# A fused linear-attention and GEGLU kernel: weight loads held back behind the DMA transposes, a re-ordered start, and four PSUM tensors for the last output tiles

## The chip, the cores and the metric

The kernel runs on one core of a Trainium2 chip. The metric is device time in microseconds (us) of one execution. "Before" and "after" are always run on the same chip in alternating rounds. An execution is slow when it takes over 1.5% more than the fastest of the same kernel in those rounds. A ratio below compares the fast runs of the two kernels in the same rounds, so it is not quite the ratio of the medians or means that are quoted beside it.

Engines in the profile: PE (matmuls) and PEld (loading of the stationary operand), DVE (vector), ACT (scalar), POOL (GpSimd, which also issues the plain loads here), SP (which issues the transposing loads and the stores).

## The reference, cut to what matters

```python
x = A_x                                            # [1, 2048, 640] bf16
g = sigmoid((x * gate_w).sum(-1, keepdims=True))
q, k, v = split_heads(x @ wqkv)                    # 32 heads of 20
phi(t)  = concat(softmax(t @ w_phi), softmax(-(t @ w_phi)))
a = (phi(q) @ (phi(k).T @ v)) / (phi(q) @ sum(phi(k)) + 1e-6) @ wo
b = (gelu(x @ w_gate) * (x @ w_up)) @ w_down       # inner width 1728
out = g * a + (1 - g) * b
```

## The kernel before

The kernel has five stages. The change touches the first and the last.

1. Start. `w_phi` is folded into the q and k weights, so that later one matmul gives `x @ Wq @ w_phi`. For this the weights are needed transposed (`wkT`, `wqT`; ten transposing DMAs on SP's queue), together with a block-diagonal matrix `BD` that PE builds from `w_phi`. `x` is transposed on PE (`xT`).
2. K/V loop over 16 tiles of 128 tokens. 3. phi(q). 4. GEGLU, 56 blocks. The output tiles of all but the last 512 tokens are made between GEGLU blocks.
5. Tail: the last four output tiles.

The loads, all issued in one go at the start (cuts are marked `...`):

```python
for k in range(NC_):   # 5 DMA transposes, then 5 more for wqT, on SP's queue
    emit_dma("sp", lambda e, k=k: e.dma_start_transpose(wkT[:, k, :], A_wqkv[:, 640+128*k : 640+128*(k+1)]), sem=s_wkT)
...
# POOL's queue, in this order: WPH, XR (x, 2 halves), masks, W1v, then without any wait
for g in range(NG):
    emit_dma("pool", lambda e, g=g, gr=gr: e.dma_start(Wo[0:gr, g, :], A_wo[120*g:120*g+gr, :]), sem=s_wo)
emit_dma("pool", ... Wgt ...); emit_dma("pool", ... Wup ...); emit_dma("pool", ... Wd ...)
```

The work of PE in the start, in program order:

```python
bd_ring = _Ring(K, "bd", 1, ["dve"])      # one PSUM slot: PA
for k in range(NC_): ...                  # BD block k: matmuls into PA, two DVE copies out
emit_xt_items(NC_ * NTG)                  # all 20 items of xT: 4 transposes, one copy (ACT or DVE)
emit_fold(wkT, W1k, extra_waits=[wkT_wait] + bd_done)   # 5 blocks of 10 matmuls, ACT copies
emit_fold(wqT, W1q, extra_waits=[wqT_wait])
```

The output tiles. Each tile `t` is: 28 "down" matmuls (`Ddown`) into PD; ACT scales PD into BSB; 12 `Wo` matmuls (`DA`) into the same PD; DVE combines PD and BSB; store.

```python
def pe_Ddown(T, tt):  w = a_ring.prod_waits(t)      # waits for DVE of the tile before
    ... e.matmul(PD[:, c0:c1], lhsT=hT[...], rhs=Wd[...])
def pe_DA(T, tt):     w = [bsb_ring.cons_wait(t)]   # waits for ACT's copy of this tile
    ... e.matmul(PD[:, c0:c1], lhsT=oT[...], rhs=Wo[...])
```

The softmax here doesn't subtract the row's maximum and nothing guards it: scores larger than these inputs give would overflow.

## Time and profile before

| | |
|---|---|
| time, median of the first 4 runs | 443.08 us (438.36 to 446.39) |
| profiled execution | 446.13 us, span 444.4 |
| first matmul of the K/V loop | 67.58 us |
| PE waits for `wqT` | 25.6 us in one piece |
| last `hT` (GEGLU done) ends | 408.98 us |
| from there to the end | 35.4 us |

The page's second part shows the span in 40 slices of 11.1 us. Digits are busy tenths; PEclk is the granted matmul clock in tenths; DMA is the mean busy share of the 16 DMA engines. Before:

```profile
PE   0681049999979989889999999999999999997875
PEclk9997559999989999999999999999999999999899
DMA  8999900000000000000000000000000000000000
```

From 33 to 67 us (digits 1, 0, 4) PE is mostly idle, while the DMA engines are busy up to 55. The chain of waits of the first 70 us (start, duration, what) says for what:

```profile
18.90 3.48 SPq L242
22.42 38.20 DMA wqT<-in_A_wqkv_dram
60.75 1.09 PE PD L388 x10
...
66.49 0.37 PE PC L465
...
67.64 1.48 PE PA L485 x10
```

The last `wqT` transpose is issued at 22.42 and takes 38.20 us to land. Then the q fold (L388) runs and the K/V loop (L485) starts. The list of waits (us in total, times, longest) names the same wait:

```profile
PE PD L388 <- DMA wqT<-in_A_wqkv_dram: 25.6, 1, 25.6
```

The chain at the end: the down matmuls of tile 12, and one whole tile out of four (the short pieces called "issue" between the lines, 0.02 to 0.05 us each, are left out):

```profile
409.12 5.76 PE PD L830 x28
...
426.49 4.09 PE PD L830 x28
430.61 0.80 ACT BSB L843
431.45 1.92 PE PD L854 x12
433.40 0.90 DVE OUT L868
434.34 4.09 PE PD L830 x28
```

A tile lasts 434.34 - 426.49 = 7.85 us and PE works for 6.01 of them. It waits for ACT (0.87) and for DVE (0.96), because all four steps use PD. The first down part took 5.76 us instead of 4.09: the granted clock was 0.5 from 410.0 to 413.4.

### The profile page before, as it was taken

To read this page: it belongs to the slowest core of one execution; us is meant where nothing else is said; L and a number is where in the kernel's file an instruction comes from. 1 tells how busy PE (TensorE), PEld (TensorE's weight loads), DVE (VectorE), ACT (ScalarE), POOL (GpSimd) and SP (SyncE) were. 2 spreads that over 40 slices of the span, in tenths; PEclk is the share of its full clock that TensorE was granted. 3 is DMA by queue.
4 is the path that set the end of the run, shared out by engine and by line. 5 is a ranking of instruction groups with operands and counts; after the bars stand their busy time and mean duration, and the time that the engine had idled before them with its cause. 6 is when DMAs were issued, how large, how long until landed. Compare 5 with 4: busy or idle time off the path is not lost.

```text
span 444.4 us, 5682 instructions
## 1 busy us (share of the span) xinstructions
PE 377.8 (85%) x2232; PEld 187.4 (42%) x2232; DVE 249.6 (56%) x333; ACT 187.2 (42%) x353; POOL 20.9 (5%) x39
## 2 busy tenths in 40 slices
PE   0681049999979989889999999999999999997875
PEld 0471045666644433333344444444444444443332
DVE  0420006999984477788999944557445574445001
ACT  1152034555536554453557744344444344441010
POOL 8900000000000000000000000000000000000000
PEclk9997559999989999999999999999999999999899
DMA  8999900000000000000000000000000000000000
GB/s 234 165 252 348 117 19 0 2 1 2 0 1 0 0 1 0 2 0 0 2 0 0 1 0 17 15 17 15 14 2 16 15 16 15 3 15 31 15 16 30
DMA packets 11434, 15.55 MB, mean 35 GB/s; under 512 B 7442, under 2 KB 9491, under 8 KB 11408
## 3 DMA queue, kind: packets, MB, share of 16 engines
q0 software_dynamic: 2384, 10.93, 8.3%
q1 hardware_dynamic: 9024, 4.26, 6.9%
q8 instruction: 18, 0.29, 0.3%
q14 instruction: 8, 0.07, 0.0%
HBM read 10.92 MB, written 2.62 MB: 30 GB/s over the span
## 4 chain that ended last, share of the span: by engine, by line
PE 66%; DVE 13%; DMA 9%; SPq 5%; issue 5%; ACT 2%; DVEq 0%
PE PD L830 15%; PE PB L754 9%; PE PA L754 9%; DMA wqT<-in_A_wqkv_dram 9%; PE PC L754 8%; PE PD L854 7%; PE PA L602 5%; DVE PHK L526 3%; DVE ZS L519 3%; SPq L242 3%; PE PA L485 3%; SPq L239 2%; DVE PHQ L640 2%; PE PB L629 2%; PE PD L696 2%
## 5 line engine op out<-in xcount | busy, mean ns | idle before, releaser
L830 PE MATMUL PD<-Wd,hT 128*128 128x512 bf16 x448 | 66.8, 304 | 5.6 <-DVE OUT L868 3.9
L808 DVE SCALAR_TENSOR_TENSOR hT<-Th,Pt 128x512 bf16<-128x512 bf16 (+1 forms) x56 | 38.4, 686 | 49.5 <-ACT Th L796 48.5
L843 ACT ACTIVATE BSB<-PD,omg 128x640 f32<-128x640 f32 x16 | 12.7, 793 | 98.8 <-PE PD L830 98.8
L830 PEld LDWEIGHTS PD<-Wd,hT 128*128 128x128 bf16 x448 | 34.6, 99 | 37.7 <-DVE OUT L868 7.2
L754 PE MATMUL PA<-xT,Wgt 128*128 128x512 bf16 (+1 forms) x190 | 47.5, 380 | 0.8 <-DVE Pt L787 0.7
L519 DVE TENSOR_REDUCE ZS<-EK 128x64 f32<-128x1280 bf16 x16 | 23.8, 1486 | 41.2 <-ACT EK L506 41.2
L754 PE MATMUL PC<-xT,Wup 128*128 128x512 bf16 (+1 forms) x185 | 46.0, 379 | 0.0
L868 DVE SCALAR_TENSOR_TENSOR OUT<-PD,gcol,BSB 128x640 bf16<-128x640 f32 x16 | 14.1, 883 | 51.2 <-PE PD L854 51.2
L640 DVE TENSOR_TENSOR PHQ<-EQ,PB 120x1024 bf16<-120x1024 bf16 (+1 forms) x24 | 29.1, 1212 | 12.7 <-PE PB L630 12.7
L796 ACT ACTIVATE Th<-Zt 128x512 bf16<-128x512 bf16 (+1 forms) x56 | 35.2, 631 | 0.0
L854 PE MATMUL PD<-Wo,oT 120*128 120x512 bf16 x192 | 30.4, 300 | 4.4 <-ACT BSB L843 4.4
L770 ACT ACTIVATE U<-PA 128x512 bf16<-128x512 f32 (+1 forms) x38 | 22.6, 595 | 23.4 <-PE PB L754 9.4
L602 PE MATMUL PA<-xT,W1q 128*120 128x512 bf16 (+1 forms) x120 | 31.2, 395 | 0.0
L673 ACT ACTIVATE NTS<-PC 120x512 bf16<-120x512 f32 (+1 forms) x24 | 14.3, 596 | 35.5 <-PE PC L654 35.5
L754 PEld LDWEIGHTS PC<-xT,Wup 128*128 128x128 bf16 (+1 forms) x185 | 18.3, 99 | 21.7
L754 PEld LDWEIGHTS PA<-xT,Wgt 128*128 128x128 bf16 (+1 forms) x190 | 16.7, 98 | 24.4 <-issue 7.9
L787 DVE SCALAR_TENSOR_TENSOR Pt<-PC,Gb 128x512 bf16<-128x512 f32 (+1 forms) x37 | 25.5, 690 | 1.3
L784 DVE SCALAR_TENSOR_TENSOR Zt<-U,PA 128x512 bf16<-128x512 bf16 (+1 forms) x38 | 25.8, 678 | 0.0
L388 PE MATMUL PD<-BD,wqT 128*128 128x120 bf16 (+1 forms) x30 | 3.1, 285 | 25.6 <-DMA wqT<-in_A_wqkv_dram 25.6
L485 PE MATMUL PA<-W1k,xT 128*128 128x512 bf16 (+1 forms) x160 | 24.5, 300 | 0.0
L495 PE MATMUL PB<-W1v,xT 128*128 128x512 bf16 (+1 forms) x160 | 24.5, 300 | 0.0
L526 DVE TENSOR_TENSOR PHK<-EK,RK 128x1280 bf16<-128x1280 bf16 x16 | 23.9, 1491 | 0.6
(114 smaller groups left out, 507.5 us busy)
## 6 DMA issues: line engine op xcount, KB each, us to landing
XR<-in_A_x_dram POOLq DMA_DIRECT2D x2, 1280.0 KB, 9.2
out_dram<-OUT SPq DMA_DIRECT2D x16, 160.0 KB, 1.8
Wgt<-in_B_w_gate_dram POOLq DMA_DIRECT2D x1, 2160.0 KB, 21.6
Wup<-in_B_w_up_dram POOLq DMA_DIRECT2D x1, 2160.0 KB, 35.4
Wd<-in_B_w_down_dram POOLq DMA_DIRECT2D x1, 2080.0 KB, 29.0
W1v<-in_A_wqkv_dram POOLq DMA_DIRECT2D x5, 160.0 KB, 9.9
Wo<-in_A_wo_dram POOLq DMA_DIRECT2D x5, 150.0 KB, 10.5
wkT<-in_A_wqkv_dram SPq DMA_TRANSPOSE x5, 11.3
```

The source lines that it names most:

```text
L485: emit("pe", lambda e, tgt=tgt, c=c, n0=n0, n1=n1, t=t: e.matmul(tgt, lhsT=xT[:, c, 128 * t:128 * (t + 1)], rhs=W1k[:, c, n0:n1], start=(c ...
L519: emit("dve", lambda e, s=s: e.tensor_reduce(ZS[:, s, :], EK[:, s, :, :].rearrange("p i (h d) -> p (i h) d", d=20), axis=AX.X, op=ALU.add) ...
L526: emit("dve", lambda e, s=s: e.tensor_tensor(PHK[:, s, :, :].rearrange("p i (h d) -> p (i h) d", d=20), EK[:, s, :, :].rearrange("p i (h d ...
L602: emit("pe", lambda e, tgt=tgt, c=c, g=g, gr=gr, T=T, last=last: e.matmul(tgt, lhsT=W1q[:, c, 120 * g:120 * g + gr], rhs=xT[:, c, 512 * T: ...
L640: emit("dve", lambda e, g=g, gr=gr: e.tensor_tensor(PHQ[0:gr, g, :, :], EQ[0:gr, g, :, :], PB[0:gr, 0:1024].rearrange("p (i n) -> p i n", ...
L754: emit("pe", lambda e, tgt=tgt, Wsrc=Wsrc, c=c, fc=fc, kr=kr, T=T: e.matmul(tgt, lhsT=Wsrc[:, c, 128 * fc:128 * fc + kr], rhs=xT[:, c, 512 ...
L784: emit("dve", lambda e, kr=kr, s=s, Gp=Gp: e.scalar_tensor_tensor(Zt[0:kr, s, :], U16[0:kr, s, :], K1, Gp, ALU.add, ALU.mult), waits=w, si ...
L787: emit("dve", lambda e, kr=kr, s=s, Up=Up: e.scalar_tensor_tensor(Pt[0:kr, s, :], Up, 0.5, Gb[0:kr, s, :], ALU.mult, ALU.mult), waits=w2, ...
L796: emit("act", lambda e, kr=kr, s=s: e.activation(Th[0:kr, s, :], Zt[0:kr, s, :], ACTF.Tanh), waits=w, sig=th_ring.prod_signal(j))
L808: emit("dve", lambda e, kr=kr, s=s, Ts=Ts, fc=fc: e.scalar_tensor_tensor(hT[0:kr, Ts, fc, :], Th[0:kr, s, :], 1.0, Pt[0:kr, s, :], ALU.add ...
L830: emit("pe", lambda e, fc=fc, kr=kr, c0=c0, c1=c1, t=t, Ts=Ts: e.matmul(PD[:, c0:c1], lhsT=hT[0:kr, Ts, fc, 128 * (t % 4):128 * (t % 4 + 1 ...
L854: emit("pe", lambda e, g=g, gr=gr, c0=c0, c1=c1, t=t: e.matmul(PD[:, c0:c1], lhsT=oT[0:gr, g, 128 * t:128 * (t + 1)], rhs=Wo[0:gr, g, c0:c ...
```

## The change

Its intent is to let the transposes land early, to keep PE fed in the start, and to overlap the last four tiles. Its core:

```diff
+        pool_op(IDENT memset, affine_select)           # moved up, XR after it
 ...
+        pool_op(lambda e: e.memset(VEXT[:, :, :, :], 1.0))     # moved up
         for g in range(NG):
-            emit_dma("pool", ... Wo ..., sem=s_wo)
+            emit_dma("pool", ... Wo ...,
+                     waits=([wqT_wait] + xr_waits if g == 0 else []), sem=s_wo)    # the gate
 ...
-        bd_ring = _Ring(K, "bd", 1, ["dve"])
+        bd_ring = _Ring(K, "bd", 2, ["dve"])           # PA and PB in turn
 ...
-        emit_xt_items(NC_ * NTG)
-        emit_fold(wkT, W1k, extra_waits=[wkT_wait] + bd_done)
-        emit_fold(wqT, W1q, extra_waits=[wqT_wait])
+        emit_xt_items(12)
+        emit_fold(wkT, W1k, extra_waits=[wkT_wait] + bd_done, cp_eng="dve", xt=(2, 2, 2, 2))
+        emit_fold(wqT, W1q, extra_waits=[wqT_wait], cp_eng="alt")   # copies ACT/DVE in turn
 ...
+        DPS = [PD, PA, PB, PC]                         # tile t: PD if t < 12, else DPS[t % 4]
-                k = CB + 14 * (T + 1) + 5 + tt * 3
+                if T < NTG - 1: k = CB + 14 * (T + 1) + 5 + tt * 3
+                else:           k = CB + NB + 3 + tt   # PE order D12 D13 A12 D14 A13 D15 A14 A15 (D: down, A: Wo)
```

Two smaller edits of the start are not in this cut: the first `xT` item now waits for the first half of `x` only, and the two PSUM slots of the `xT` items lie in PA and PB instead of both in PB.

POOL issues in order, so a wait ahead of the first `Wo` load holds back `Wo`, `Wgt`, `Wup` and `Wd`, 7.3 MB by the sizes that the profile lists (7,280 KB).

More of the change, by code (lines that the diff above doesn't have):

```diff
@@ L245, in bass_gated_mix__linear_kernel_hedgehog__geglu_ffn__prompt_kernel, with _xr_dma @@
         wqT_wait = s_wqT.final()
-        emit_dma("pool", lambda e: e.dma_start(WPH[0:20, :, :], A_w_phi.rearrange("h i f -> i h f")), sem=s_wph)
-        wph_wait = s_wph.final()
-        for hlf in range(2):
+        def _xr_dma(hlf):
             emit_dma("pool", lambda e, hlf=hlf: e.dma_start(
@@ L252, in bass_gated_mix__linear_kernel_hedgehog__geglu_ffn__prompt_kernel @@
                 x2[1024 * hlf:1024 * (hlf + 1), :].rearrange("(n p) d -> p n d", p=128)), sem=s_xr[hlf])
-        xr_waits = [s_xr[0].final(), s_xr[1].final()]
+        emit_dma("pool", lambda e: e.dma_start(WPH[0:20, :, :], A_w_phi.rearrange("h i f -> i h f")), sem=s_wph)
+        wph_wait = s_wph.final()
+        xr_waits = [(s_xr[0].h, 16), (s_xr[1].h, 16)]
+        pool_op(lambda e: e.memset(IDENT[:, :], 1.0))
+        pool_op(lambda e: e.affine_select(IDENT[:, :], IDENT[:, :], pattern=[[-1, 128]], compare_op=ALU.is_equal,
+                                        fill=0.0, base=0, channel_multiplier=1))
+        ident_wait = (s_pool.h, pool_cnt[0])
+        _xr_dma(0)
+        _xr_dma(1)
         pool_op(lambda e: e.memset(Zb[:, :], 1.0))
@@ L257, in bass_gated_mix__linear_kernel_hedgehog__geglu_ffn__prompt_kernel @@
         pool_op(lambda e: e.memset(ZERO20[:, :], 0.0))
+        zero_wait = (s_pool.h, pool_cnt[0])
         pool_op(lambda e: e.memset(BlkOnes[:, :, :], 1.0))
@@ L266, in bass_gated_mix__linear_kernel_hedgehog__geglu_ffn__prompt_kernel @@
         pool_op(lambda e: e.memset(CHALF[:, :], 0.5))
-        pool_op(lambda e: e.memset(IDENT[:, :], 1.0))
-        pool_op(lambda e: e.affine_select(IDENT[:, :], IDENT[:, :], pattern=[[-1, 128]], compare_op=ALU.is_equal,
-                                        fill=0.0, base=0, channel_multiplier=1))
         masks_wait = (s_pool.h, pool_cnt[0])
@@ L279, in bass_gated_mix__linear_kernel_hedgehog__geglu_ffn__prompt_kernel @@
         w1v_wait = s_w1v.final()
+        pool_op(lambda e: e.memset(VEXT[:, :, :, :], 1.0))
+        vext_init_wait = (s_pool.h, pool_cnt[0])
         for g in range(NG):
             gr = _grows(g)
-            emit_dma("pool", lambda e, g=g, gr=gr: e.dma_start(Wo[0:gr, g, :], A_wo[120 * g:120 * g + gr, :]), sem=s_wo)
+            emit_dma("pool", lambda e, g=g, gr=gr: e.dma_start(Wo[0:gr, g, :], A_wo[120 * g:120 * g + gr, :]),
+                     waits=([wqT_wait] + xr_waits if g == 0 else []), sem=s_wo)
         wo_wait = s_wo.final()
@@ L289, in bass_gated_mix__linear_kernel_hedgehog__geglu_ffn__prompt_kernel, with emit_xt_items, xt_ready_waits @@
         wd_wait = s_wd.final()
-        bd_ring = _Ring(K, "bd", 1, ["dve"])
+        xp_ring = _Ring(K, "xp", 2, ["act", "dve"])
+        XPS = [PA[:, 0:256].bitcast(BF16), PB[:, 0:256].bitcast(BF16)]
+        xt_item = [0]
+        def emit_xt_items(n):
+            for _ in range(n):
+                i = xt_item[0]
+                if i >= NC_ * NTG:
+                    return
+                xt_item[0] += 1
+                q, c = i // NC_, i % NC_
+                slot = XPS[i % 2]
+                ceng = "act" if i % 2 == 0 else "dve"
+                w = [(xp_ring.done[ceng][i % 2].h, i // 2)] if i >= 2 else []
+                if i == 0:
+                    w = w + [xr_waits[0], ident_wait] + bd_done_ref
+                if i == 10:
+                    w = w + [xr_waits[1]]
+                for n4 in range(4):
+                    n = 4 * q + n4
+                    sig = xp_ring.prod_signal(i) if n4 == 3 else None
+                    emit("pe", lambda e, slot=slot, n=n, c=c, n4=n4: e.transpose(
+                        slot[:, 128 * n4:128 * (n4 + 1)], XR[:, n, 128 * c:128 * (c + 1)], IDENT[:, :]),
+                         waits=(w if n4 == 0 else []), sig=sig)
+                if ceng == "act":
+                    emit("act", lambda e, slot=slot, q=q, c=c: e.activation(xT[:, c, 512 * q:512 * (q + 1)], slot, ACTF.Copy),
+                         waits=[xp_ring.cons_wait(i)], sig=xp_ring.cons_signal(i, "act"))
+                else:
+                    emit("dve", lambda e, slot=slot, q=q, c=c: e.tensor_copy(xT[:, c, 512 * q:512 * (q + 1)], slot),
+                         waits=[xp_ring.cons_wait(i)], sig=xp_ring.cons_signal(i, "dve"))
+        def xt_ready_waits(q):
+            last = 5 * q + 4
+            ws = []
+            for sl, ceng in ((0, "act"), (1, "dve")):
+                items = [i for i in range(last + 1) if i % 2 == sl]
+                if items:
+                    ws.append((xp_ring.done[ceng][sl].h, len(items)))
+            return ws
+        bd_ring = _Ring(K, "bd", 2, ["dve"])
+        bd_done_ref = []
         for k in range(NC_):
-            lo, hi = (PA[:, 0:512], PA[:, 512:1024])
+            lo, hi = (PA[:, 0:512], PA[:, 512:1024]) if k % 2 == 0 else (PB[:, 0:512], PB[:, 512:1024])
             r0, r1 = 128 * k, 128 * (k + 1)
@@ L326, in bass_gated_mix__linear_kernel_hedgehog__geglu_ffn__prompt_kernel, with emit_fold @@
         bd_done = bd_ring.finals_done("dve")
-        xp_ring = _Ring(K, "xp", 2, ["act", "dve"])
-        XPS = [PB[:, 0:256].bitcast(BF16), PB[:, 512:768].bitcast(BF16)]
-        xt_item = [0]
-        def emit_xt_items(n):
-            for _ in range(n):
-                i = xt_item[0]
-                if i >= NC_ * NTG:
-                    return
-                xt_item[0] += 1
-                q, c = i // NC_, i % NC_
-                slot = XPS[i % 2]
-                ceng = "act" if i % 2 == 0 else "dve"
-                w = [(xp_ring.done[ceng][i % 2].h, i // 2)] if i >= 2 else []
-                if i == 0:
-                    w = w + xr_waits + [masks_wait]
-                for n4 in range(4):
-                    n = 4 * q + n4
-                    sig = xp_ring.prod_signal(i) if n4 == 3 else None
-                    emit("pe", lambda e, slot=slot, n=n, c=c, n4=n4: e.transpose(
-                        slot[:, 128 * n4:128 * (n4 + 1)], XR[:, n, 128 * c:128 * (c + 1)], IDENT[:, :]),
-                         waits=(w if n4 == 0 else []), sig=sig)
-                if ceng == "act":
-                    emit("act", lambda e, slot=slot, q=q, c=c: e.activation(xT[:, c, 512 * q:512 * (q + 1)], slot, ACTF.Copy),
-                         waits=[xp_ring.cons_wait(i)], sig=xp_ring.cons_signal(i, "act"))
-                else:
-                    emit("dve", lambda e, slot=slot, q=q, c=c: e.tensor_copy(xT[:, c, 512 * q:512 * (q + 1)], slot),
-                         waits=[xp_ring.cons_wait(i)], sig=xp_ring.cons_signal(i, "dve"))
-        def xt_ready_waits(q):
-            last = 5 * q + 4
-            ws = []
-            for sl, ceng in ((0, "act"), (1, "dve")):
-                items = [i for i in range(last + 1) if i % 2 == sl]
-                if items:
-                    ws.append((xp_ring.done[ceng][sl].h, len(items)))
-            return ws
-        emit_xt_items(NC_ * NTG)
-        fd_ring = _Ring(K, "fd", 2, ["act"])
+        bd_done_ref.extend(bd_done)
+        fd_ring = _Ring(K, "fd", 2, ["cp"])
         fi = [0]
-        def emit_fold(src, dst, extra_waits=()):
+        def emit_fold(src, dst, extra_waits=(), cp_eng="act", xt=()):
             for cm in range(NC_):
+                eng_ = cp_eng if cp_eng != "alt" else ("act" if cm % 2 == 0 else "dve")
                 i = fi[0]
@@ L390, in emit_fold @@
                          waits=(w if j == 0 else []), sig=sig)
-                emit("act", lambda e, lo=lo, cm=cm, dst=dst: e.activation(dst[:, cm, 0:480], lo[:, 0:480], ACTF.Copy),
-                     waits=[fd_ring.cons_wait(i)])
-                emit("act", lambda e, hi=hi, cm=cm, dst=dst: e.activation(dst[:, cm, 480:640], hi[:, 0:160], ACTF.Copy),
-                     sig=fd_ring.cons_signal(i, "act"))
-        emit_fold(wkT, W1k, extra_waits=[wkT_wait] + bd_done)
-        emit_fold(wqT, W1q, extra_waits=[wqT_wait])
+                if eng_ == "act":
+                    emit("act", lambda e, lo=lo, cm=cm, dst=dst: e.activation(dst[:, cm, 0:480], lo[:, 0:480], ACTF.Copy),
+                         waits=[fd_ring.cons_wait(i)])
+                    emit("act", lambda e, hi=hi, cm=cm, dst=dst: e.activation(dst[:, cm, 480:640], hi[:, 0:160], ACTF.Copy),
+                         sig=fd_ring.cons_signal(i, "cp"))
+                else:
+                    emit("dve", lambda e, lo=lo, cm=cm, dst=dst: e.tensor_copy(dst[:, cm, 0:480], lo[:, 0:480]),
+                         waits=[fd_ring.cons_wait(i)])
+                    emit("dve", lambda e, hi=hi, cm=cm, dst=dst: e.tensor_copy(dst[:, cm, 480:640], hi[:, 0:160]),
+                         sig=fd_ring.cons_signal(i, "cp"))
+                if cm < len(xt):
+                    emit_xt_items(xt[cm])
+        emit_xt_items(12)
+        emit_fold(wkT, W1k, extra_waits=[wkT_wait] + bd_done, cp_eng="dve", xt=(2, 2, 2, 2))
+        foldk_done = [(fd_ring.done["cp"][0].h, fd_ring.done["cp"][0].count), (fd_ring.done["cp"][1].h, fd_ring.done["cp"][1].count)]
+        emit_fold(wqT, W1q, extra_waits=[wqT_wait], cp_eng="alt")
         xT_all_waits = xt_ready_waits(3)
         xT_wait = xT_all_waits[0]
-        fold_done = fd_ring.finals_done("act")
+        fold_done = fd_ring.finals_done("cp")
         dbg_dump("xT0", xT[:, 0, 0:512], xt_ready_waits(3))
         dbg_dump("BD3", BDt[:, 3, :], bd_done)
-        dbg_dump("W1k0", W1k[:, 0, :], fold_done)
+        dbg_dump("W1k0", W1k[:, 0, :], foldk_done)
         dbg_dump("W1v1", W1v[:, 1, :], [w1v_wait])
@@ L407, in bass_gated_mix__linear_kernel_hedgehog__geglu_ffn__prompt_kernel @@
         dbg_dump("wkTall", wkT[:, :, :].rearrange("p a b -> p (a b)"), [wkT_wait])
-        dbg_dump("W1q2", W1q[:, 2, :], fold_done)
+        dbg_dump("W1q2", W1q[:, 2, :], foldk_done)
         EQ = PHQ = NTS = DTE = RD = None
-        pool_op(lambda e: e.memset(VEXT[:, :, :, :], 1.0))
-        vext_init_wait = (s_pool.h, pool_cnt[0])
-        pk_wait_init = fold_done + bd_done
+        pk_wait_init = foldk_done + bd_done + xt_ready_waits(3)
         pkready = _Ring(K, "pk", 2, [])
@@ L465, in bass_gated_mix__linear_kernel_hedgehog__geglu_ffn__prompt_kernel @@
         emit("pe", lambda e: e.matmul(PC[0:40, 0:512], lhsT=Zb[0:20, 0:40], rhs=ZERO20[0:20, 0:512], start=True, stop=False),
-             waits=pk_wait_init)
+             waits=fold_done)
         emit("pe", lambda e: e.matmul(PC[0:120, 512:1024], lhsT=Zb[0:20, 0:120], rhs=ZERO20[0:20, 0:512], start=True, stop=False))
@@ L730, in bass_gated_mix__linear_kernel_hedgehog__geglu_ffn__prompt_kernel, with dslot, dlidx @@
         dh_sems = [_Sem(K, f"dh{u}") for u in range(2)]
-        dn_ring = _Ring(K, "dn", 1, [])
-        bsb_ring = _Ring(K, "bsb", 1, [])
-        a_ring = _Ring(K, "aa", 1, ["dve"])
+        DPS = [PD, PA, PB, PC]
+        def dslot(t):
+            return 0 if t < 12 else (t % 4)
+        def dlidx(t):
+            return sum(1 for u in range(t) if dslot(u) == dslot(t))
+        dn_rings = [_Ring(K, f"dn{q}", 1, []) for q in range(4)]
+        bsb_rings = [_Ring(K, f"bsb{q}", 1, []) for q in range(4)]
+        a_rings = [_Ring(K, f"aa{q}", 1, ["dve"]) for q in range(4)]
         o16_ring = _Ring(K, "o16", 2, [])
@@ L814, in pe_Ddown @@
             Ts = T % 2
-            w = a_ring.prod_waits(t)
+            q = dslot(t)
+            li = dlidx(t)
+            PX = DPS[q]
+            w = a_rings[q].prod_waits(li)
             if tt == 0:
@@ L819, in pe_Ddown @@
                     w = w + [wd_wait, wo_wait] + oT_done
+            if q >= 1 and li == 0:
+                for s_ in range(2):
+                    w.append((gu_ring.done["act"][s_].h, gu_ring.done["act"][s_].count))
+                    w.append((gu_ring.done["dve"][s_].h, gu_ring.done["dve"][s_].count))
             first = True
@@ L826, in pe_Ddown @@
                     if last:
-                        sig = dn_ring.prod_signal(t)
+                        sig = dn_rings[q].prod_signal(li)
                     elif fc == NFC - 1 and seg == 0 and tt == 3:
                         sig = (dh_sems[Ts].h, dh_sems[Ts].plan_inc())
-                    emit("pe", lambda e, fc=fc, kr=kr, c0=c0, c1=c1, t=t, Ts=Ts: e.matmul(
-                        PD[:, c0:c1], lhsT=hT[0:kr, Ts, fc, 128 * (t % 4):128 * (t % 4 + 1)], rhs=Wd[0:kr, fc, c0:c1],
+                    emit("pe", lambda e, fc=fc, kr=kr, c0=c0, c1=c1, t=t, Ts=Ts, PX=PX: e.matmul(
+                        PX[:, c0:c1], lhsT=hT[0:kr, Ts, fc, 128 * (t % 4):128 * (t % 4 + 1)], rhs=Wd[0:kr, fc, c0:c1],
                         start=(fc == 0), stop=(fc == NFC - 1)), waits=(w if first else []), sig=sig)
@@ L837, in act_D @@
             s = t % 2
-            w = [dn_ring.cons_wait(t)]
+            q = dslot(t)
+            li = dlidx(t)
+            PX = DPS[q]
+            w = [dn_rings[q].cons_wait(li)]
             if t >= 2:
-                w.append((a_ring.done["dve"][0].h, t - 1))
+                q2 = dslot(t - 2)
+                w.append((a_rings[q2].done["dve"][0].h, dlidx(t - 2) + 1))
             if t == 0:
                 w.append(gcol_wait)
-            emit("act", lambda e, s=s, t=t: e.activation(BSB[:, s, :], PD[:, 0:640], ACTF.Copy, scale=omg[:, t:t + 1]),
-                 waits=w, sig=bsb_ring.prod_signal(t))
+            emit("act", lambda e, s=s, t=t, PX=PX: e.activation(BSB[:, s, :], PX[:, 0:640], ACTF.Copy, scale=omg[:, t:t + 1]),
+                 waits=w, sig=bsb_rings[q].prod_signal(li))
         def pe_DA(T, tt):
             t = 4 * T + tt
-            w = [bsb_ring.cons_wait(t)]
+            q = dslot(t)
+            li = dlidx(t)
+            PX = DPS[q]
+            w = [bsb_rings[q].cons_wait(li)]
             first = True
@@ L853, in pe_DA @@
                     last = (g == NG - 1 and seg == 1)
-                    emit("pe", lambda e, g=g, gr=gr, c0=c0, c1=c1, t=t: e.matmul(
-                        PD[:, c0:c1], lhsT=oT[0:gr, g, 128 * t:128 * (t + 1)], rhs=Wo[0:gr, g, c0:c1],
+                    emit("pe", lambda e, g=g, gr=gr, c0=c0, c1=c1, t=t, PX=PX: e.matmul(
+                        PX[:, c0:c1], lhsT=oT[0:gr, g, 128 * t:128 * (t + 1)], rhs=Wo[0:gr, g, c0:c1],
                         start=(g == 0), stop=(g == NG - 1)), waits=(w if first else []),
-                         sig=(a_ring.prod_signal(t) if last else None))
+                         sig=(a_rings[q].prod_signal(li) if last else None))
                     first = False
@@ L862, in dve_D @@
             s = t % 2
-            w = [a_ring.cons_wait(t)]
+            q = dslot(t)
+            li = dlidx(t)
+            PX = DPS[q]
+            w = [a_rings[q].cons_wait(li)]
             if t == 0:
@@ L867, in dve_D @@
                 w.append((s_out[s].h, 16 * (t // 2)))
-            emit("dve", lambda e, s=s, t=t: e.scalar_tensor_tensor(
-                OUT16[:, s, :], PD[:, 0:640], gcol[:, t:t + 1], BSB[:, s, :], ALU.mult, ALU.add),
-                 waits=w, sig=a_ring.cons_signal(t, "dve"))
-            o16_ring.ready[s].count = max(o16_ring.ready[s].count, t // 2 + 1)
+            emit("dve", lambda e, s=s, t=t, PX=PX: e.scalar_tensor_tensor(
+                OUT16[:, s, :], PX[:, 0:640], gcol[:, t:t + 1], BSB[:, s, :], ALU.mult, ALU.add),
+                 waits=w, sig=a_rings[q].cons_signal(li, "dve"))
         def sp_out(t):
             s = t % 2
-            w = [(a_ring.done["dve"][0].h, t + 1)]
+            q = dslot(t)
+            w = [(a_rings[q].done["dve"][0].h, dlidx(t) + 1)]
             emit_dma("sp", lambda e, s=s, t=t: e.dma_start(out2[128 * t:128 * (t + 1), :], OUT16[:, s, :]),
@@ L885, in bass_gated_mix__linear_kernel_hedgehog__geglu_ffn__prompt_kernel @@
             for tt in range(4):
-                k = CB + 14 * (T + 1) + 5 + tt * 3
+                if T < NTG - 1:
+                    k = CB + 14 * (T + 1) + 5 + tt * 3
+                else:
+                    k = CB + NB + 3 + tt
                 dsteps.setdefault(k, []).append((T, tt))
@@ L937, in bass_gated_mix__linear_kernel_hedgehog__geglu_ffn__prompt_kernel @@
         dbg_dump("oT0", oT[0:120, 0, 0:1024], oT_done_dump)
-        fin_w = [(a_ring.done["dve"][0].h, NT_), (hT_sems[NTG - 1].h, NFC)]
+        fin_w = [(a_rings[3].done["dve"][0].h, dlidx(NT_ - 1) + 1), (hT_sems[NTG - 1].h, NFC)]
         dbg_dump("hT", hT[:, 1, 0:4, :].rearrange("p a b -> p (a b)"), fin_w)
```

## The prediction

> **What bounds it now.** Span 444.4 us. From the chain of waits and the timeline of the profiled run:
> - Start, to 67.6 us. The chain is the ten DMA transposes on SP's queue: issues run until 22.4, and the last wqT lands 38.2 us after its issue, at 60.6. PE idles from 35.7 to 60.75 (25.6 us, its largest single wait). Then five wqT folds and ACT copies; the first K matmul starts at 67.58.
> - K/V loop (to about 131), phi(q) (to 213), GEGLU (to 409, PE 98% busy): the diff leaves them alone.
> - Tail, 409.1 to 444.4: four output tiles in one PSUM tensor. A tile takes 7.86 us: down matmuls 4.09, ACT copy and hand-overs 0.85, Wo matmuls 1.92, DVE combine and hand-overs 1.0. PE waits inside every tile. The first down part took 5.74: granted clock 0.5 from 410.1 to 413.5.
>
> **Why wqT is late.** Uncontended, a transpose took 3.0 us from issue to landing, and they ran about 1.7 us apart by the packet records. Once Wo, Wgt, Wup and Wd (7.2 MB) were issued, from 14.9 on, wqT landed at about 27, 42, 43, 56 and 61. The Trainium skill, "DMA: Bandwidth & Descriptors", section "Issuing engines are not separate DMA queues", says that DMAs of all issuers share the same 16 engines and interleave. The trace agrees: DMA is about 90% busy to 55 us while the transposes crawl.
>
> **What the change does.**
> 1. Wo, Wgt, Wup, Wd wait for wqT and XR. Transposes then share only with XR (as now) and W1v (0.8 MB). About 4,870 of 6,400 transpose packets remain when XR lands at 14.0; at 640 per 1.7 us that is 13 us, plus 3 for W1v. Estimate: wqT lands at 30 (26 to 38). Weights then load until about 60; Wgt is first needed at 213.
> 2. BD gets two PSUM slots: 1.9 us a block falls to about 1.0, so BD ends near 15 instead of 19.
> 3. Eight x transposes go between the wkT folds, whose copies move to DVE; wqT copies alternate. PE has work until about 32.6 (12 items at 0.65, five folds at 1.0, eight items at 0.5), so a landing before that does not bind. The q fold takes 6; first K matmul near 39.5. Gain 28 us, all on the chain. Without the gate, points 2 and 3 would gain almost nothing.
> 4. Tail: tiles 12 to 15 use four PSUM tensors, in PE order D12, D13, A12, D14, A13, D15, A14, A15. ACT and DVE latencies are hidden except at the end: 5.7 + 3 x 3.9 + 4 x 1.8 = 24.6 us, instead of 32.1 to the last Wo matmul. Gain 7.5 us. Its start does not move: tile 12 still waits for the last hT.
>
> **Time.** 446.1 (the profiled run) - 28 - 7.5 = 410.6; runs scatter from 438 to 446, perhaps partly from the wqT landing. I say 409 us, range 402 to 417. Faster by over 2%: 0.97; within 2%: 0.02; slower: 0.01.
>
> **What would show it.** Last wqT landing at 26 to 38; PE idle before the q fold under 5 us; first K matmul at 37 to 43; no 27 us low-clock stretch before it (the skill's "TensorE: Matmul & The Clock Gate", section "What's actually happening", calls half clock after an idle window the default; here 0.5 from 38 to 65); weights landed near 60; last hT to the end about 28 us instead of 35.4; the stretches between unchanged within 2 us.
>
> **What would make it wrong.** Transposes limited by something other than the loads (their packets averaged about 100 ns in the last 5 us, with little else running), so wqT lands after 40; weight loads disturbing the K/V loop; interleaved folds slower than the sum; PE throttled in the denser tail.

## The result, and the profile after

After: 406.49 us median (405.33 to 413.22, 11 runs). Before: 443.81 us median (438.3 to 450.61, 16 runs). The ratio of fast runs is 0.9213, with a 95% interval of 0.9175 to 0.9251. The profiled execution after took 405.85 us (span 404.1) and is a fast one, while that of before is a slow one. So the difference of the two traces (40.3 us) is larger than the 35 or so between fast runs.

The slices after:

```profile
PE   0798999997998989899999999999999999998896
PEclk9998999998999999999999999999999999999999
DMA  7999900000000000000000000000000000000001
```

The hole in PE is gone. The chain of waits at the start no longer contains the transfer of a DMA (some of its pieces):

```profile
22.54 0.43 PE PB L319 x4
22.97 1.06 PE PC L400 x10
24.05 0.66 DVE W1k L409
...
31.82 0.51 PE PD L400 x10
32.35 0.57 ACT W1q L404
33.27 0.37 PE PC L484
...
34.61 2.79 PE PA L504 x10
```

L400 is the fold, L319 an `xT` item, L504 the first K matmul. What waits for `wqT` now is only POOL, which is the gate:

```profile
POOL Wo L288 <- DMA wqT<-in_A_wqkv_dram: 11.6, 1, 11.6
```

The chain at the end:

```profile
377.48 4.07 PE PD L864 x28
381.54 4.01 PE PA L864 x28
385.56 1.84 PE PD L895 x12
387.39 4.01 PE PB L864 x28
391.41 1.84 PE PA L895 x12
393.24 4.01 PE PC L864 x28
397.26 1.84 PE PB L895 x12
399.09 1.85 PE PC L895 x12
400.95 0.03 issue
400.97 0.88 DVE OUT L912
```

PE runs without a gap. In both traces the same points cut the span; "landing" is read from the trace's landing records, the others from the timeline:

| us | before | after |
|---|---|---|
| last `wqT` lands | 60.6 | 27.3 |
| first K matmul | 67.6 | 34.5 |
| from there to the first numerator matmul of phi(q) | 71.2 | 72.6 |
| from there to the first `hT` | 78.45 | 78.45 |
| first to last `hT` (starts) | 191.1 | 191.1 |
| start of the last `hT` to the end | 36.09 | 27.45 |

So 33 us came from the start, 8.6 from the tail, and the K/V stretch gave 1.4 back.

### The profile page after: what moved, and what is told of

Its sections match the earlier page's. It is cut to its first block, busy times and chain, and to the rows that moved or that the text cites. A ratio compares the mean times of both kernels' runs of the same rounds, so it can differ in the third digit from the quotient of the medians.

```text
span 404.1 us, 5693 instructions
## 1 busy us (share of the span) xinstructions
PE 372.0 (92%) x2232; PEld 182.6 (45%) x2232; DVE 255.0 (63%) x347; ACT 182.0 (45%) x339; POOL 20.8 (5%) x39
## 4 chain that ended last, share of the span: by engine, by line
PE 73%; DVE 16%; issue 5%; ACT 3%; POOL 2%; DVEq 0%; POOLq 0%
PE PD L864 13%; PE PB L781 10%; PE PA L781 10%; PE PC L781 9%; PE PD L895 6%; PE PA L621 5%; DVE PHK L545 3%; DVE ZS L538 3%; PE PA L504 3%; DVE PHQ L659 2%; PE PB L648 2%; PE PD L715 2%; ACT EK L525 1%; DVE RK L541 1%; PE PC L476 1%
## 5 line engine op out<-in xcount | busy, mean ns | idle before, releaser
L864 PE MATMUL PD<-Wd,hT 128*128 128x512 bf16 (+1 forms) x364 | 52.9, 299 | 2.6 <-DVE hT L835 1.7
L881 ACT ACTIVATE BSB<-PD,omg 128x640 f32<-128x640 f32 x13 | 10.3, 793 | 75.9 <-PE PD L864 75.9
L864 PEld LDWEIGHTS PD<-Wd,hT 128*128 128x128 bf16 (+1 forms) x364 | 27.8, 98 | 27.7 <-issue 3.4
L659 DVE TENSOR_TENSOR PHQ<-EQ,PB 120x1024 bf16<-120x1024 bf16 (+1 forms) x24 | 29.1, 1212 | 12.9 <-PE PB L649 12.9
L912 DVE SCALAR_TENSOR_TENSOR OUT<-PD,gcol,BSB 128x640 bf16<-128x640 f32 x13 | 11.5, 884 | 31.6 <-PE PD L895 31.6
L692 ACT ACTIVATE NTS<-PC 120x512 bf16<-120x512 f32 (+1 forms) x24 | 14.3, 596 | 35.5 <-PE PC L673 35.5
L781 PEld LDWEIGHTS PA<-xT,Wgt 128*128 128x128 bf16 (+1 forms) x190 | 16.7, 98 | 24.4 <-issue 7.9
L504 PE MATMUL PA<-W1k,xT 128*128 128x512 bf16 (+1 forms) x160 | 25.8, 311 | 0.0
L895 PE MATMUL PD<-Wo,oT 120*128 120x512 bf16 (+1 forms) x156 | 24.7, 300 | 0.9 <-ACT BSB L881 0.9
L514 PE MATMUL PB<-W1v,xT 128*128 128x512 bf16 (+1 forms) x160 | 24.6, 301 | 0.0
L545 DVE TENSOR_TENSOR PHK<-EK,RK 128x1280 bf16<-128x1280 bf16 x16 | 23.9, 1492 | 0.6
L524 ACT ACTIVATE EK<-PA 128x640 bf16<-128x640 f32 x16 | 11.2, 703 | 27.6 <-PE PA L504 27.6
## 6 DMA issues: line engine op xcount, KB each, us to landing
wkT<-in_A_wqkv_dram SPq DMA_TRANSPOSE x5, 11.7
```

The costliest lines, as they stand in the source:

```text
L504: emit("pe", lambda e, tgt=tgt, c=c, n0=n0, n1=n1, t=t: e.matmul(tgt, lhsT=xT[:, c, 128 * t:128 * (t + 1)], rhs=W1k[:, c, n0:n1], start=(c ...
L545: emit("dve", lambda e, s=s: e.tensor_tensor(PHK[:, s, :, :].rearrange("p i (h d) -> p (i h) d", d=20), EK[:, s, :, :].rearrange("p i (h d ...
L659: emit("dve", lambda e, g=g, gr=gr: e.tensor_tensor(PHQ[0:gr, g, :, :], EQ[0:gr, g, :, :], PB[0:gr, 0:1024].rearrange("p (i n) -> p i n", ...
L781: emit("pe", lambda e, tgt=tgt, Wsrc=Wsrc, c=c, fc=fc, kr=kr, T=T: e.matmul(tgt, lhsT=Wsrc[:, c, 128 * fc:128 * fc + kr], rhs=xT[:, c, 512 ...
L864: emit("pe", lambda e, fc=fc, kr=kr, c0=c0, c1=c1, t=t, Ts=Ts, PX=PX: e.matmul(PX[:, c0:c1], lhsT=hT[0:kr, Ts, fc, 128 * (t % 4):128 * (t ...
L895: emit("pe", lambda e, g=g, gr=gr, c0=c0, c1=c1, t=t, PX=PX: e.matmul(PX[:, c0:c1], lhsT=oT[0:gr, g, 128 * t:128 * (t + 1)], rhs=Wo[0:gr, ...
```

## The experiments

Theory A: the gate brings `wqT` early, and the other edits of the start only shorten PE's own work behind it. Rival B: the gain of the start comes from the moved `xT` items, the two BD slots and the copies on DVE. All outputs are right.

### The kernel before, again

No edit.

> The kernel before, unchanged, to get a profile of another execution, if possible a fast one. Theory: the scatter of its times (438 to 451) comes from when the last wqT transpose lands, because nothing else differs between executions; then a fast execution shows wqT landing 5 to 8 us earlier than 60.6, and the stretches after the first K matmul are equal within 1 us. Rival: the scatter comes from the matmul clock in the later stretches; then wqT lands at 60 to 61 again and the length from the first K matmul to the end differs instead.

Two executions: 446.51 (profiled, slow) and 439.49. The profiled one landed `wqT` at 58.7, which is 1.9 us earlier than in the first trace, and still took as long: its stretch from the first K matmul to phi(q) lasted 74.0 us instead of 71.2, with the granted clock at 0.5 from 37.4 to 71.6, which is into the K/V loop, and again from 129.6 to 136.4. So both the landing and the clock move the time by microseconds. An execution of about 439 us was not profiled, so what makes those is open. The record has their mean granted clocks, 0.953 and 0.968, from which we estimate some 42 and 28 us at half clock; but a longer wait for `wqT` adds half-clock time as well, so this does not separate the two.

### The gate alone

```diff
 (kernel before)
+        pool_op(VEXT memset)        # ahead of the wait, as in the changed kernel
-            emit_dma("pool", ... Wo ..., sem=s_wo)
+            emit_dma("pool", ... Wo ..., waits=([wqT_wait] + xr_waits if g == 0 else []), sem=s_wo)
```

> The kernel before with the gate alone: Wo, Wgt, Wup, Wd wait for wqT and XR (and the VEXT fill stands before that wait). Theory A (the gate brings wqT early; the other start edits only shorten PE's own work): wqT lands at 26 to 29, PE has no wait for it since the x transposes and the wkT fold run to 35 to 36, first K matmul at 41 to 43, time about 420. Rival B (the start gain comes from the moved x transposes, the BD slots and the copies on DVE): first K matmul stays later than 60 and the time within 3 us of before.

419.31 us median (418.06 to 420.05), ratio 0.9459 (0.9385 to 0.9533). `wqT` landed at 27.7 and the first K matmul was at 40.8. PE waited for no transpose; its longest wait is the one for the masks at the very start:

```profile
PE PA L314 <- POOL IDENT L268: 9.7, 1, 9.7
```

Theory A holds, and B falls as the main cause: the gate alone gives 24.2 us (fast means 443.39 and 419.18).

### Everything but the gate

```diff
 (kernel after)
-                     waits=([wqT_wait] + xr_waits if g == 0 else []), sem=s_wo)
+                     sem=s_wo)
```

> The changed kernel without the gate, all else kept. Theory A: wqT lands at 52 to 61 again, PE waits 25 us or more for it, first K matmul 6 us after the landing, only the tail's 7 to 8.6 us remain of the gain: time 431 to 438. Rival B: first K matmul near 35 to 42 and time below 415.

438.93 us median, ratio 0.9908 (0.9815 to 1.0001), just above the 431 to 438 that were expected. `wqT` landed at 59.9, and PE's longest wait is back:

```profile
PE PD L400 <- DMA wqT<-in_A_wqkv_dram: 31.0, 1, 31.0
```

The first K matmul was at 66.7. Since the tail alone gives at least as much (4.5 us here by the fast means, 6.3 in the next run), no gain is left for the re-ordered start without the gate: PE only reaches its wait sooner and waits longer.

### The tail alone

The kernel before, with the tail hunks of the change.

> The kernel before with the tail edits alone. If the two parts add up: from the first down matmul of tile 12 to the end about 26.6 to 28.3 us instead of 35.3, and 7 to 8.6 us less than before at equal state, ratio 0.980 to 0.984. If the tail gain of the profile (8.65) owed 1.67 us to a clock window that fell well by chance, the gain here may be 7 only.

437.15 us median, ratio 0.9864 (0.9778 to 0.9949), 6.3 us by the fast means, which is unclear at 2%. The interval reaches from about 2 to 10 us, so the time alone does not size the gain; the trace does. From the start of the last `hT` to the end it took 29.1 us. Here the first down part again fell into a half-clock window:

```profile
407.74 5.74 PE PD L845 x28
413.49 4.01 PE PA L845 x28
```

Before it was 36.1 with such a window, so the overlap is worth 7.0 us. The 8.6 of the first pair of traces contains about 1.7 (5.74 - 4.07) of luck with the clock. All the profiles but that of the mixed form below fall into this pattern: the old tail takes 34.4 us, or 36.1 with the window on its first part, and the new one 27.4 to 27.5, or 29.1.

### The start alone

The kernel after, with the tail of before.

> The changed kernel with the tail of before (all start edits kept). If the parts add up: first K matmul at 34 to 35 as in the changed kernel, from the last hT to the end 34.4 us (36.1 if the first down part falls in a half-clock window) instead of 27.4, so 7 to 8.7 us more than the changed kernel: 413 to 415. If the start edits and the tail edits overlapped in what they gain, it would stay below 410.

413.58 us median (413.46 to 413.65), ratio 0.9325 (0.9293 to 0.9358). First K matmul at 34.7, and 34.4 us from the last `hT` to the end, against 27.4 in the changed kernel: 7.0 us. The two parts add up.

### Four PSUM tensors in the old PE order

```diff
 (kernel after)
-                if T < NTG - 1: k = CB + 14 * (T + 1) + 5 + tt * 3
-                else:           k = CB + NB + 3 + tt
+                k = CB + 14 * (T + 1) + 5 + tt * 3
```

> The changed kernel with its four PSUM tensors in the tail but the old PE order (down 12, Wo 12, down 13, Wo 13, and so on). Theory: the gain has two shares, the DVE wait that the tensors take away (about 1.0 us a tile, three tiles) and the ACT wait that the order takes away (0.85 to 0.9 us a tile, four tiles). Then the last hT to the end is about 31 us, half-way between 27.4 and 34.4, and the time 409.5 to 410.5. Rival: the tensors alone give it all (27 to 28 us, 406 to 407), or the order alone does (34 us, 413).

409.93 us median, ratio 0.9248 (0.9208 to 0.9288), and 31.3 us from the last `hT` to the end. The chain (again without the "issue" pieces):

```profile
384.30 4.03 PE PA L864 x28
388.35 0.80 ACT BSB L881
389.20 1.91 PE PA L895 x12
391.11 4.03 PE PB L864 x28
```

The wait for DVE is gone, since the next tile has its own tensor; the wait for ACT stays, since a tile's Wo matmuls come right after its down matmuls. Each share is about half of the 7 us (34.4, 31.3, 27.4). The opposite test, the new order in one tensor, is not possible: D13 would wait for a combine of tile 12 whose Wo matmuls stand behind D13 in PE's order.

### The gate in front of Wd only

```diff
 (kernel after)
-            ... Wo ..., waits=([wqT_wait] + xr_waits if g == 0 else []), sem=s_wo)
+            ... Wo ..., sem=s_wo)
-        emit_dma("pool", ... Wd[:, 0:13, :] ..., sem=s_wd)
+        emit_dma("pool", ... Wd[:, 0:13, :] ..., waits=[wqT_wait] + xr_waits, sem=s_wd)
```

> The changed kernel with the gate moved from Wo to Wd: Wo, Wgt and Wup (5.2 MB) are free to run beside the transposes, Wd (2.2 MB) waits. Theory A (wqT is late in proportion to the bytes that run beside it): without the gate 7.4 MB delay it by about 33 us, 4.5 us per MB, so 5.2 MB delay it by 23: wqT lands near 50 (47 to 53), first K matmul near 56, time 425 to 430. Rival (any load in flight starves the transposes until all loads that were issued are done): Wo, Wgt and Wup alone hold it to the end of their own transfers, and wqT lands with or right after the last of them. Rival 2: a part of the loads does no harm and wqT lands before 35.

429.66 us median (426.46 to 430.2), ratio 0.9673 (0.9621 to 0.9725). `wqT` landed at 50.7, the first K matmul was at 57.4:

```profile
PE PD L401 <- DMA wqT<-in_A_wqkv_dram: 21.0, 1, 21.0
```

The number fits the proportion to the bytes, but it fits the rival too: `Wup`, the last free load, landed at 50.3, just before `wqT`. Before, the last `Wd` landed at 60.4 and `wqT` at 60.6. In all five profiles in which loads ran free, `wqT` landed 0.3 to 1.0 us after the last of them. The packet counts show how both can fit. For the kernel before, the DMA view of 33 to 45 us, where both kinds were pending (queue, packets, MB, share of the 16 engines):

```profile
q0 software_dynamic: 703, 4.07, 93.8%
q1 hardware_dynamic: 714, 0.17, 8.2%
```

q0 carries POOL's loads, q1 SP's transposes. They advance one packet for one packet: 703 against 714. In this run, 27 to 45 us, it is 662 against 650. But a load packet moves 5.8 KB and a transpose packet 0.24 KB, so the loads get 93.8% of the engines' time.

Near the end, from 56.3 to 58.8 us, the shares add up to two engines' work, and the packet records alternate: one transpose packet of 256 bytes (18 ns), one load packet of 5,120 bytes (214 ns).

```profile
q0 software_dynamic: 22, 0.11, 11.8%
q1 hardware_dynamic: 22, 0.01, 1.0%
```

(This is the DMA view of that stretch.) So there the last transpose ends together with the last load. One for one is not the whole account, though. From 14 to 61 us q1 moved 4,204 packets and q0 1,807, and from 48 to 54 us, where the loads took only 11.7% of the engines' time, the transposes crawled all the same: 348 packets in 6 us, by our estimate one in 0.28 us for each of 16 engines. That is near the pace of the engines that still alternate (a pair in about 0.23 us), as if all waited for the slowest; this was not tested. The Trainium skill, "DMA: Bandwidth & Descriptors", section "Queues, rings and completion order", states such an arbitration: each engine round-robins between the queue rows that have work, at packet granularity. The equal counts and the alternation agree with it; the crawl from 48 to 54 us is not explained by it. No run here changed the packet size, so the mechanism is read from counts and not isolated.

### A version further along

```diff
 (kernel after)
-            w = bd_ring.prod_waits(k) + ([wph_wait, masks_wait] if k == 0 else [])
+            w = bd_ring.prod_waits(k) + ([wph_wait, zero_wait] if k == 0 else [])  # 3rd mask of 6
-        (five W1v loads, without a wait, ahead of the VEXT memset)
+        (after it, the first with waits=[wqT_wait] + xr_waits, which then is the gate for all)
-        (four matmuls that zero PC and PD ahead of the K/V loop, waits=fold_done)
+        (the same after the first K and V tile)
```

> A version further along: the BD blocks wait for their own masks only, the W1v loads too wait for wqT, and the four zeroing matmuls of the kv accumulators stand after the first K and V tile. In the changed kernel wqT (27.0) came before PE was ready for it (28.4), and PE was held by its own chain from 9.6 on. Expected: first BD matmul at 6.5 instead of 9.6, wqT landing at 24 to 25 since W1v no longer shares, first K matmul at 29.5 to 31.5 instead of 34.5, time 402 to 404. If W1v then comes too late, the first V matmul waits for it instead.

399.35 us. `wqT` landed at 21.0 and the first K matmul was at 29.0. The transposes gained more than expected: 0.8 MB of W1v beside them had cost 6 us (the other two edits of this run issue no DMA). With next to nothing beside them, the DMA view of 15 to 21 us shows:

```profile
q1 hardware_dynamic: 3312, 0.81, 73.9%
q0 software_dynamic: 96, 0.00, 1.1%
```

That is 3,312 transpose packets in 6 us, against 714 in 12 us in the kernel before.

### Four kernels timed together

The changed kernel again, the version above, and two more. The first of them takes the q fold off the start: it runs in half blocks inside the K/V loop, in a PSUM bank freed by moving the kv sums of the last head group to a half-empty bank.

```diff
 (version above)
-        emit_fold(wqT, W1q, extra_waits=[wqT_wait], cp_eng="alt")
 ...                                      # in the K/V loop over tiles t
+            if 1 <= t <= 10: emit_qfold(t - 1)        # half a block, into PC[:, 0:480]
+            if 1 <= t <= 10: emit_qcopy(t - 1)        # ACT
```

The second gives the `xT` items four PSUM slots instead of two.

```diff
 (version above)
-        xp_ring = _Ring(K, "xp", 2, ["act", "dve"])
-        XPS = [PA[:, 0:256].bitcast(BF16), PB[:, 0:256].bitcast(BF16)]
+        xp_ring = _Ring(K, "xp", 4, ["act", "dve"])
+        XPS = [PA[:, 0:256] ..., PB[:, 0:256] ..., PA[:, 512:768] ..., PB[:, 512:768] ...]
```

> The changed kernel again, on the same chip and in the same rounds as the three versions below, so that they compare directly: 405 to 407 us in fast runs.

> The version of the earlier look (BD on its own masks, W1v behind wqT, zeroing after the first K and V tile), timed. The look gave 399.35, wqT at 20.9, first K matmul at 29.0. Expected 398.5 to 400.5, that is 6 to 7 us under the changed kernel of the same rounds.

> The same with the wqT fold taken off the start: it runs in ten half blocks inside the K/V loop, in a PSUM bank freed for it. The first K matmul then follows the wkT fold, near 26 instead of 29.0. The K/V loop pays for the fold's 2.6 to 3.3 us of matmuls if PE bounds it, and less if PE's waits for DVE there take it up (PE was busy 58.8 of 63 us of the loop before). Expected: the stretch from the first K matmul to the first NT matmul 71.6 plus 0 to 3, time 396 to 400. If PE bounds the loop fully, equal to the version without it.

> The version of the look with four PSUM slots for the x transposes instead of two. In the look a pair of items took 1.30 us, of which PE waited 0.26 for ACT's copy of 0.60. Expected: a pair in 1.0 to 1.1 us, the first wkT fold 1 to 1.5 us earlier, first K matmul at 27.5 to 28.5, time 398 to 399.5. If the folds between are bound by DVE's copies instead, nothing is gained.

The last two columns, in us, are of the one profiled execution of each.

| kernel | median us (range) | ratio to before (95%) | first K matmul | from there to phi(q) |
|---|---|---|---|---|
| changed kernel | 407.36 (405.77 to 411.75) | 0.916 (0.909 to 0.923) | 38.1 | 73.2 |
| version further along | 400.05 (399.35 to 400.11) | 0.9 (0.8943 to 0.9057) | 29.4 | 70.3 |
| with the q fold in the loop | 400.64 (399.96 to 404.98) | 0.9038 (0.8963 to 0.9112) | 27.3 | 73.6 |
| with four `xT` slots | 398.39 (397.58 to 399.56) | 0.8968 (0.8909 to 0.9027) | 26.7 | 71.7 |

The changed kernel's profile here is of its 411.75 us execution, and it shows where the 6 us to the first trace come from. Its chain contains

```profile
6.53 17.88 DMA wkT<-in_A_wqkv_dram
24.45 1.11 PE PC L400 x10
...
38.18 2.25 PE PA L504 x5
```

`wkT` landed 1.5 us later than in the first trace (24.4 against 22.9), and the folds then ran in the half clock: 0.93 us for ten matmuls instead of 0.56, until the clock came up at 30.0 instead of 23.9. The first K matmul slid from 34.5 to 38.1, the half-clock window on it lasted 6.8 us instead of 3.4, and a further one at 152.9, which the first trace does not have, lengthened phi(q) by 1.7 (80.1 against 78.4). The expectation of 405 to 407 held for two of six executions; the others were 407.27, 407.45, 411.2 and 411.75.

Taking the q fold into the loop is a miss in effect. The loop starts 2.1 us earlier, but it lasts 3.3 us longer in these two profiles, of which the clock has a share (mean 0.98 against 1.00 by the stretch view). The earlier look at the version without it had the same mean clock in the loop, 0.98, and took 71.7 us, so about 1.9 is the fold's. PE is busy for 70.6 of 73.6 us there, against 66.1 of 70.3: PE has little idle time in the loop that could take up the fold.

Four slots gave a time inside the expected 398 to 399.5, and an earlier first K matmul than expected: a pair of items takes 0.43 + 0.43 us instead of 1.30, and the first K matmul comes 2.7 us earlier than in the version above. The clock, which came up at 18.2 instead of 22.0, has a share in that; the runs do not separate it. This is the fastest kernel: 398.39 us, a tenth under the kernel before. Against the changed kernel of the same rounds, the fast means are 398.48 and 408.28.

## Why the prediction was right

It said 409 us (402 to 417). Measured: 406.49. Point by point:

- `wqT` at 30 (26 to 38): 27.3. The sum behind it was lucky in its parts. 13 us were put down for 4,870 packets and 3 us for W1v. But 2,516 of the 6,400 packets had run before 14.0 in the kernel before, so about 3,900 were left. When W1v was taken away, about as many took 7.0 us after XR's landing (14.0 to 21.0), so W1v had cost 6.3 (27.3 - 21.0). One term was too large and the other too small. The transposes are faster alone and suffer more from a neighbour than was assumed.
- "Without the gate, points 2 and 3 would gain almost nothing": shown by the run without the gate.
- "PE has work until about 32.6, so a landing before that does not bind": right in kind, since PE reached the q fold at 28.4 and `wqT` had landed at 27.3. But the size was off. The fold with two `xT` items took 1.13 us a block, not 2.0, because the clock was full there: ten matmuls in 0.56 (from the last wkT block to the first wqT block, 27.82 to 28.38) where the prediction took 1.0 from the kernel before. The first K matmul came at 34.5 instead of 39.5, and the gain of the start was 33 instead of 28.
- The 1.0 was read from a stretch in which PE ran at half clock. The clock row of the page shows full clock there, but the record of clock changes begins only at 34.5 us in that trace, and the durations before it tell otherwise: in the timeline the block that starts at 33.46 takes 1.10 us and the next one, at 34.48, takes 0.67 for the same ten matmuls. The q fold's block at 61.68, where the record does say half clock, takes 1.10 too.
- Not foreseen: the half-clock window from 34.1 to 37.5 in the trace after. The first K tile's ten matmuls took 2.85 us instead of 1.53. This is most of the 1.4 us that the K/V stretch gave back. "No 27 us low-clock stretch" was right.
- The tail, 7.5 us: 7.0 by the runs that do it alone or undo it. The 8.6 of the first pair of traces had 1.7 of clock in it.
- Stretches between unchanged within 2 us: 1.4, 0.0 and 0.0. The weights landed at 52, not 60: they took 24.6 us from the opening of the gate at 27.6, where 30 were put down.
- "Runs scatter from 438 to 446, perhaps partly from the wqT landing": not settled by the kernel before run again. A landing still counts in the changed kernel, as `wkT` did in the 411.75 us execution, and the half-clock windows come on top.
- The total of 410.6 was formed from a slow execution. That its gain of 35.5 (28 + 7.5) meets the 35 or so between fast runs is in part luck: it was worked out against the slow trace, and the two traces differ by 40.3. Fast to fast, the change is worth about 35 us: about 24 by the gate, about 6 by the re-ordered start once the gate is there (419.18 against 413.57 by fast means of different rounds), and about 6 to 7 by the tail. Which of the start's edits (the two BD slots, the moved `xT` items, the copies on DVE, the earlier start of `xT`) gave the 6 us was not separated.

## What to carry to other kernels

Loads that nobody needs soon are not free when a transposing DMA that everybody waits for runs beside them; put a wait in front of them and look at the packet counts of the two queues. An edit that shortens the work ahead of a wait is worth nothing until the wait itself moves, and the same edit was worth about 6 us once it had. When you take a duration from a profile to cost a new schedule, check at which matmul clock it ran, by comparing equal instructions in neighbouring stretches.

## What the Trainium skill lacked or had wrong

- "DMA: Bandwidth & Descriptors", "Rules for kernel authors", says that "A transpose next to ordinary DMAs needs nothing". That may hold for correctness. For time it does not: beside 7.3 MB of loads the last transpose landed at 60.6 us, behind a gate at 27.3, and with W1v held back too at 21.0. The page states the packet-wise arbitration, but not what follows for a queue of 0.24 KB packets beside one of 5.8 KB packets (714 to 703 packets in 12 us, 8.2% to 93.8% of the time).
- The same page, "Latency and other measured facts", gives 261 GB/s as the effective bandwidth of a DMA transpose in one kernel. Here, almost alone on the engines, 0.81 MB in 6 us is 135 GB/s. The page's figure is for one kernel with a non-contiguous middle dimension, and the transposes filled only 73.9% of the engines' time here, so this does not refute it; it did not carry over to these transposes of 160 KB each.
- "TensorE: Matmul & The Clock Gate", "What's actually happening", calls the ramp less than 1% of a typical span. Here the ramp at the start of the K/V loop and later half-clock windows, of 3.4 us or multiples of it, moved one stretch of the same work between 69.9 us (gate alone, no window) and 74.0 us (kernel before, again), and the tail by 1.7 us. That is enough to hide a 1% effect in a single trace.
- The same page, "Part 4: PE-mode transpose", says that the full clock does not engage for transposes. The runs agree in one half: with four `xT` slots the transposes ran back to back from 12.4 to 17.5 us at 107 ns each, and the clock came up only at 18.2. But once it was up, the same transposes ran at full clock: four in 0.22 us, 55 ns each, from 18.31 to 18.53.
- No page says that the record of the granted clock can begin late in a trace (at 34.5 us in the kernel before), so that the page shows full clock where durations show half.
